# The last tile's second and third column groups stored by one transfer per queue

## The chip, the cores and the metric

The kernel runs on one core of one Trainium2 chip. The metric is the device time of one execution in microseconds (us), as the median of several runs. Beside it stands the span of a profiled execution, from its first to its last instruction; it is about 1.8 us shorter than the time of the same run. The document also uses a third measure, the **tail**: from the end of the last copy out of PSUM to the end of the span, read from the trace.

## The reference

An attention without softmax feeds a gated feed-forward block:

```python
scores = scale * np.matmul(q, k.transpose(0, 1, 3, 2))     # 8 x 12 heads, 448 x 64
attn   = np.maximum(scores, 0.0) ** 2 / S
x      = (attn @ v), heads side by side                     # 3584 x 768
out    = (gelu(x @ w_gate) * (x @ w_val)) @ w_out           # 768 -> 1536 -> 768, float32
```

Only the last step matters here. Its output, 3584 rows of 768 columns, is made in 28 tiles of 128 rows; a tile holds two chunks of 64 rows.

## The kernel before

A planner in the kernel lists operations per engine with their dependencies and emits them in the order of a simulated clock. The part that the change touches makes one column group of one output tile: 48 matmuls into a PSUM bank, a copy to SBUF (`osb`), and the stores. An ordinary tile has two groups of 384 columns; the last tile (`last`) has three, of 384, 192 and 192.

```python
def add_out(at, t, g):
    last = 2 * t + 2 == B * SC
    bounds = (0, OGS, OGS + OGS // 2, 2 * OGS) if last else (0, OGS, 2 * OGS)
    cols = slice(bounds[g], bounds[g + 1])
    ...                                             # matmuls
    def emit_store(j, engine, cols):                # 64 rows of chunk j
        b, c = chunks[j]
        rows = out[b * S:(b + 1) * S, :].rearrange("(p c) d -> c p d", c=SC)
        engine.dma_start(rows[c, :, cols], osb[t][HALF[j], cols])
    ...
    cp = Op("DVE" if last else "ACT", 0.48, emit_copy, [ops[1][-1]], prio=1)
    ...
    if last:
        SP.append(Op("SP", 0.6, lambda: emit_store(0, nc.sync, cols), [cp], prio=-1))
        ACT.append(Op("ACT", 0.1, lambda: emit_store(1, nc.scalar, cols), [cp], prio=-1))
    elif g == NG - 1:
        SP.extend(Op("SP", 0.6, lambda j=j: emit_store(j, nc.sync, slice(0, d_model)), [cp], prio=-1)
                  for j in range(2))
```

So the last tile is stored by six transfers: after each group's copy one from SyncE's queue (SP, chunk 0) and one from ScalarE's queue (ACT, chunk 1), 96, 48 and 48 KB each. An *issue* is what an engine's sequencer, which takes the engine's instructions in order, does to start a transfer; SPq and ACTq in the views below are the sequencers of SyncE and ScalarE. A transfer has *landed* when its semaphore, a counter that the program can wait for, says so.

## Time and profile before

| | before |
|---|---|
| time, median of 3 runs | 429.53 us (429.22 to 430.35) |
| span of the profiled run | 427.8 us |
| TensorE busy | 421.0 us (98%) |
| end of the last matmul / of the last copy | 423.61 / 423.99 us |
| tail (last copy to end of span) | 3.79 us |

The table is read from the bottom. TensorE is busy nearly throughout, so the body is matmul work. The change cannot touch it; it works in the 3.79 us after the last copy, in which the last stores are issued, move their data and land, and the program closes. The prediction shows the lines of this stretch. One more view belongs to them: what SyncE's sequencer waited for from 420 us on (waiter, releaser: us in total, times, longest).

```profile
...
SPq L560 <- DVE osb L555: 2.2, 1, 2.2
SPq L728 <- DMA out_dram<-osb: 1.3, 3, 0.5
SPq L728 <- PEq L728: 0.7, 2, 0.5
```

L728 is the line of the launch; instructions under it are the closing steps that the program adds after the kernel's own. SyncE stands there waiting for landings of `out_dram`, so the landing of the last store and not an engine's work is what the end waits for.

### The profile page before, as it was taken

Reading aid. Unit: us, or ns where it says so; the run is one execution under the profiler, and the core shown is the slowest. Engines: PE = TensorE matmul, PEld = TensorE weight load, DVE = VectorE, ACT = ScalarE, POOL = GpSimd, SP = SyncE. Lnnn points to the kernel's source line nnn. Section 1 sums busy time; section 2 is a strip of 40 time slices with the busy share of each in tenths; the row PEclk is TensorE's granted clock in tenths of the full one; section 3 lists DMA queues with packets and bytes.
Section 4 is the critical chain, followed back from the end, with each engine's and each line's share of the span. In section 5 each row is a group of like instructions: output and inputs, shape, how many; then the busy total and the mean of one; then the engine's idle time right before and its main releaser. Section 6 shows DMA issues by size and latency. Waiting matters only on the chain.

```text
span 427.8 us, 19598 instructions
## 1 busy us (share of the span) xinstructions
PE 421.0 (98%) x9090; PEld 359.3 (84%) x9093; DVE 213.1 (50%) x347; ACT 223.6 (52%) x320; POOL 71.5 (17%) x116
## 2 busy tenths in 40 slices
PE   8999999999999999999999999999999999999996
PEld 3556788789998888889999988979999988977895
DVE  3965766367653665346643566445743555212201
ACT  4946674366655555556465565555546555322220
POOL 7655320012200132012300123011310000000000
PEclk9999999999999999999999999999999999999998
DMA  7999999988964389545975379735984100120034
GB/s 103 190 199 198 201 209 192 139 126 109 121 128 89 47 114 116 118 83 81 133 119 113 48 92 130 149 63 57 137 142 96 38 4 3 48 69 3 2 77 113
DMA packets 75377, 44.91 MB, mean 105 GB/s; under 512 B 36128, under 2 KB 71840, under 8 KB 75296
## 3 DMA queue, kind: packets, MB, share of 16 engines
q0 software_dynamic: 37088, 24.39, 42.1%
q1 hardware_dynamic: 37968, 19.08, 25.9%
q8 instruction: 71, 1.16, 1.2%
q10 hardware_dynamic: 240, 0.20, 0.2%
q14 instruction: 10, 0.08, 0.1%
HBM read 48.76 MB, written 11.01 MB: 140 GB/s over the span
## 4 chain that ended last, share of the span: by engine, by line
PE 96%; DMA 1%; POOL 1%; issue 1%; ACT 0%; DVE 0%; ACTq 0%; POOLq 0%
PE ff L159 86%; PE sp L159 8%; DMA qk<-in_k_dram 1%; PE sp L342 1%; POOL qk L211 1%; PE ff L304 1%; ACT rl L389 0%; PE ff L342 0%; DVE osb L555 0%; POOL ident masks.py:199 0%; POOL ident masks.py:197 0%; ACTq L389 0%; POOLq L717 0%
## 5 line engine op out<-in xcount | busy, mean ns | idle before, releaser
L159 PE MATMUL ff<-xT,wg 64*64 64x448 bf16 x2304 | 217.7, 349 | 0.0
L159 PE MATMUL ff<-xT,wv 64*64 64x448 bf16 x2304 | 216.7, 349 | 0.3 <-issue 0.2
L389 ACT ACTIVATE rl<-sp 128x896 bf16<-128x896 f32 x168 | 152.4, 918 | 94.1 <-PE sp L159 77.2
L159 PE MATMUL ff<-wo,uT 64*64 64x384 bf16 (+1 forms) x2736 | 151.6, 320 | 0.0
L159 PEld LDWEIGHTS <-wv 64*64 64x64 bf16 x2304 | 126.6, 107 | 17.5 <-issue 2.7
L159 PEld LDWEIGHTS <-wg 64*64 64x64 bf16 x2304 | 126.5, 107 | 16.6 <-issue 0.6
L395 DVE TENSOR_TENSOR attnT<-rl 128x896 bf16<-128x896 bf16 x168 | 103.8, 622 | 69.3 <-ACT rl L389 68.2
L159 PEld LDWEIGHTS <-uT 64*64 64x64 bf16 x2736 | 126.8, 107 | 5.1 <-issue 0.3
L159 PE MATMUL sp<-qkT 64*64 64x448 bf16 (+1 forms) x768 | 108.3, 328 | 0.5 <-ACT rl L389 0.4
L503 DVE TENSOR_TENSOR uT<-gel,ff 128x448 bf16<-128x448 bf16 x96 | 59.5, 620 | 79.3 <-PE ff L159 68.8
L159 PE MATMUL ff<-attnT,v 64*64 64x448 bf16 (+1 forms) x768 | 86.0, 326 | 0.1
L498 ACT ACTIVATE gel<-ff 128x448 bf16<-128x448 f32 x96 | 52.1, 543 | 55.2 <-PE ff L159 54.7
L159 PEld LDWEIGHTS <-qkT 64*64 64x64 bf16 x768 | 44.2, 106 | 9.6 <-issue 4.2
L159 PEld LDWEIGHTS <-v 64*64 64x64 bf16 x768 | 46.5, 107 | 5.3 <-issue 1.3
L555 ACT COPY osb<-ff 128x384 f32<-128x384 f32 x54 | 25.7, 476 | 46.6 <-PE ff L159 44.0
L448 DVE TENSOR_SCALAR xT<-ff 128x448 bf16<-128x448 f32 x48 | 29.9, 623 | 31.8 <-PE ff L159 31.7
L211 POOL DMA_DIRECT2D qk<-in_q_dram x25 | 15.5, 622 | 129.3 <-DVE uT L503 121.7
L224 POOL DMA_DIRECT2D v<-in_v_dram x44 | 27.3, 627 | 41.5 <-DVE uT L503 32.0
L211 POOL DMA_DIRECT2D qk<-in_k_dram x25 | 15.4, 615 | 64.0 <-DVE uT L503 55.7
L258 DVE COPY qkr<-qk 128x1792 bf16<-128x1792 bf16 x18 | 19.3, 1077 | 0.0
L555 DVE COPY osb<-ff 128x192 f32<-128x192 f32 (+1 forms) x3 | 1.2, 420 | 18.3 <-PE ff L159 18.3
L342 PEld LDWEIGHTS <-qk 128*64 128x64 bf16 x168 | 5.2, 110 | 3.8 <-issue 3.5
(23 smaller groups left out, 43.9 us busy)
## 6 DMA issues: line engine op xcount, KB each, us to landing
out_dram<-osb SPq DMA_DIRECT2D x54, 192.0 KB, 2.8
v<-in_v_dram POOLq DMA_DIRECT2D x42, 128.0 KB, 4.4
qk<-in_q_dram POOLq DMA_DIRECT2D x23, 224.0 KB, 4.3
qk<-in_k_dram POOLq DMA_DIRECT2D x23, 224.0 KB, 5.1
wg<-in_moe_w_gate_dram POOLq DMA_DIRECT2D x6, 384.0 KB, 10.5
wv<-in_moe_w_val_dram POOLq DMA_DIRECT2D x6, 384.0 KB, 11.3
wo<-in_moe_w_out_dram POOLq DMA_DIRECT2D x4, 576.0 KB, 15.5
v<-in_v_dram POOLq DMA_DIRECT2D x2, 384.0 KB, 11.2
```

Source lines behind the costliest of these rows:

```text
L159: return nc.tensor.matmul(o, lhsT, rhs, start=start, stop=stop, tile_position=(P * row, P * col))
L211: op = load(4 * (h1 - h0) * S * D, lambda: nc.gpsimd.dma_start(tile_of().rearrange("p (h x) -> p h x", h=H)[:, h0:h1, :], src[b, h0:h1].re ...
L224: return nc.gpsimd.dma_start(v16[b][HALF[i], h0:h1, :, :], v[b, h0:h1].rearrange("h (p c) d -> p h c d", c=SC)[:, :, c0:c0 + VC, :])
L258: nc.vector.tensor_copy(qkr[b][:, m], qk16[b].rearrange("p (h c d) -> p c h d", c=SC, d=D)[:, :, 4 * m:4 * m + 4])
L304: nc.tensor.matmul(t[:, :], warm[:, 0:128], warm[:, :], start=True, stop=True)
L342: nc.tensor.transpose(t[HALF[j], c, :], src[:, 2 * (2 * m + r) + j, c, :], ident[:, :], tile_position=(0, P * j))
L389: nc.scalar.activation(rl[:, :, :], box[0][:, :, 0:S], AF.Relu)
L395: nc.vector.tensor_tensor(a[:, :, :], box[1][:, :, :], box[1][:, :, :], op=ALU.mult)
L448: nc.vector.tensor_scalar_mul(xT[b][:, pr, :], box[0][:, 0:S], scalar1=out_scale)
L498: nc.scalar.activation(gel[b, fc][:, :], box[0][:, 0:S], AF.Gelu)
L503: u_op[b, fc].ins = nc.vector.tensor_tensor(uT[b][:, fc, :], gel.pop((b, fc))[:, :], box[0][:, 0:S], op=ALU.mult).ins
L555: (nc.vector.tensor_copy if last else nc.scalar.copy)(osb[t][:, cols], box[0][:, 0:N])
```

## The change

Intent: with one issue less per queue at the end, the last store should leave earlier. The first group is stored as before; the second is not stored on its own, and its columns go out with the third's.

```diff
-        if last:
-            SP.append(Op("SP", 0.6, lambda: emit_store(0, nc.sync, cols), [cp], prio=-1))
-            ACT.append(Op("ACT", 0.1, lambda: emit_store(1, nc.scalar, cols), [cp], prio=-1))
-        elif g == NG - 1:
+        if last and g != 1:
+
+            part = slice(bounds[g and g - 1], bounds[g + 1])
+            SP.append(Op("SP", 0.6, lambda: emit_store(0, nc.sync, part), [cp], prio=-1))
+            ACT.append(Op("ACT", 0.1, lambda: emit_store(1, nc.scalar, part), [cp], prio=-1))
+        elif g == NG - 1 and not last:
```

## The prediction

> **What bounds the kernel now.** I read the page first, then the chain of waits near the end, the timeline of the last five microseconds cut into short windows, the DMA issues of the same windows, and the trace's records of single DMA packets.
>
> ```profile
> span 427.8 us, 19598 instructions
> PE 421.0 (98%) x9090; PEld 359.3 (84%) x9093; DVE 213.1 (50%) x347; ACT 223.6 (52%) x320; POOL 71.5 (17%) x116
> ```
>
> TensorE is busy for 421.0 of 427.8 us, so the body is bound by it. The change does not touch the body; only what follows the last matmul can move. The chain of waits in the window 423 to 428 us (start, us, what):
>
> ```profile
> 422.99 0.62 PE ff L159 x15
> 423.61 0.02 issue
> 423.63 0.36 DVE osb L555
> ```
>
> The last 15 matmuls end at 423.61, the last PSUM copy (192 columns, third group) ends at 423.99, and the chain view stops there. The span ends at 427.77, 3.78 us later, and all of that is the last stores and the program's closing steps. The timeline of this stretch (start, us, engine) and, below it, the DMA issues:
>
> ```profile
> 422.77 0.56 DVE L555 COPY osb<-ff 128x384 f32<-128x384 f32 x1 [18.27 <-PE ff L159]
> ...
> 423.25 0.35 DVE L555 COPY osb<-ff 128x192 f32<-128x192 f32 x1
> ...
> 423.36 0.47 SPq L560 DMA_DIRECT2D out_dram<-osb  x1
> 423.36 0.56 ACTq L560 DMA_DIRECT2D out_dram<-osb  x1
> ...
> 423.63 0.36 DVE L555 COPY osb<-ff 128x192 f32<-128x192 f32 x1
> ...
> 423.92 0.54 SPq L560 DMA_DIRECT2D out_dram<-osb  x1
> ...
> 424.01 0.73 ACTq L560 DMA_DIRECT2D out_dram<-osb  x1
> ...
> 424.56 0.55 SPq L560 DMA_DIRECT2D out_dram<-osb  x1
> 424.83 0.56 ACTq L560 DMA_DIRECT2D out_dram<-osb  x1
> ```
> ```profile
> out_dram<-osb SPq DMA_DIRECT2D x1, 96.0 KB, 2.1
> out_dram<-osb ACTq DMA_DIRECT2D x1, 96.0 KB, 2.4
> ...
> out_dram<-osb SPq DMA_DIRECT2D x1, 48.0 KB, 1.9
> out_dram<-osb ACTq DMA_DIRECT2D x1, 48.0 KB, 2.0
> ```
> ```profile
> L728 SPq EVENT_SEMAPHORE  x4: 17/22/28, 426.8 to 427.7; - x4
> ```
>
> The thing to see is the gap between the copies and the issues. The three copies end at 423.33, 423.60 and 423.99. The first pair of issues follows its copy by 0.03 us. The second copy, though, has been done since 423.60 while the second issues begin at 423.92 (SP) and 424.01 (ACT), each when its sequencer has finished the one before. The third pair is later still: its copy ended at 423.99, but SP issues at 424.56 (0.57 us late) and ACT at 424.83 (0.84 us late). One issue costs a sequencer 0.47 to 0.73 us plus some 0.1 us before the next, while the last two copies come only 0.28 and 0.39 us after their predecessors. Two queues with three issues each therefore cannot keep up. ACT's third store is last: issued at 424.83, 2.0 us to landing. SyncE's wait for it ends at 426.8, and from there 0.97 us of closing semaphores lead to 427.77.
>
> **What the Trainium skill says.** "DMA: Bandwidth & Descriptors", section "Issuing engines are not separate DMA queues": transfers begun from several engines run on the same 16 DMA engines and interleave, and a second issuing engine saves only the sequencer's time to issue. This is the quantity at stake here, and 0.47 to 0.73 us an issue is not small beside a 48 KB transfer. The same page, "Queues, rings and completion order": SP and ACT own one row of rings each, and an engine takes the descriptors of a ring in order. The packet records agree: ACT's second transfer sends its first packet at 425.416, just after its first transfer's last has ended at 425.402; SP's does so at 425.230 after 425.151. The same page, "Anatomy of one DMA", gives about 2.0 us fixed plus bytes over 436 GB/s, most of the fixed part being the receipt of the write; it is written for the other issue path. Here 48 KB takes 1.9 to 2.0 us, which fits the sum, but not its split: the third stores wait 1.22 us (SP) and 1.23 us (ACT) from issue to first packet, and ACT's landing is seen 0.37 us after its last packet ended at 426.437. "Perfetto Trace Analysis", "DMA Instruction — HWDGE": an issue's profiled span runs from satisfied semaphores to the free sequencer, and the movement of data comes outside it. The trace agrees: ACT's third issue ends at 425.39, its packets start at 426.06.
>
> **The change part by part.** Removed: the second group's two issues, one on SP and one on ACT. A comparison of the built instruction streams shows one issue less on each, and no other instruction moved or changed. Copies, matmuls and the first group's stores stay. The last issue now moves 384 columns (96 KB) instead of 192 (48 KB).
>
> 1. *Earlier issue.* SP is free at 423.83 and ACT at 423.92, both before the last copy ends at 423.99. With the 0.03 us seen between the first copy and its issue, both begin at about 424.03 (up to 424.06). For ACT that is 424.83 - 424.03 = 0.80 us earlier, for SP 0.53 us. The second group's data leaves some 0.1 us later than before on SP, and this does not matter.
>
> 2. *Later start of data within the transfer.* From 424.03, 1.23 us to the first packet gives 425.26. On SP its first transfer's packets end at 425.15, so SP starts at about 425.26. On ACT the first transfer's packets occupy the ring to 425.40, so ACT starts at about 425.42, not 425.26. Before, the first packet of ACT's last store was at 426.06; the gain at this point has shrunk from 0.80 to 0.64 us.
>
> 3. *Twice the data at the end.* Two 96 KB transfers now run beside each other. The first group's pair is the same case already measured: first packet 424.483, last end 425.402, so 0.92 us for both, the second having joined 0.45 us late. Its 128 data packets have median lengths of 0.111 (SP) and 0.065 us (ACT), so 64 x 0.111 + 64 x 0.065 = 11.3 us of engine time, or 0.70 us over 16 engines if none idles. My estimate for the new pair is therefore 0.70 to 0.92 us after 425.26, an end of the last packet between 425.96 and 426.18, against 426.44 before. Of the 0.64 us, 0.26 to 0.48 us remain.
>
> 4. *Landing and close.* Plus 0.37 us to the seen landing: 426.33 to 426.55 in place of 426.80. Check by the other route: ACT's 96 KB store of the first group took 2.4 us from issue to landing, and 424.03 + 2.4 = 426.43. The 0.97 us of closing semaphores remain. Two landings less to wait for saves nothing, because those waits were passed earlier.
>
> Sum: -0.80 (issue) + 0.16 (ring still in use) + about 0.27 (more data) = -0.37 us. The span becomes 427.4, and the time 429.53 - 0.37 = 429.16, which I round to 429.15: a gain of 0.09%.
>
> **The rivals.** *The larger transfer gives all of it back.* If two 96 KB transfers together took as long as a full 192 KB store (median 2.8 us to landing in the page's DMA list), landing would be at 424.03 + 2.8 = 426.83, and the time would stay at 429.5. For it: the packets of the first pair were longer than those of 48 KB (0.111 and 0.065 against 0.036 to 0.053 us). Against it: the full stores come two behind each other on one queue, 384 KB in all; here the pair is 192 KB and half of it on each queue. I give this 15%.
>
> *The whole issue gain stays.* If the data were hidden and landing took 2.0 us as for 48 KB, landing would be at 426.03 and the time at 428.76. For it: SP's 96 KB store took only 2.1 us, and the DMA engines were only half busy from 425.5 on. Against it: ACT's took 2.4 us, and the kernel ends with the later of the two. I give 15%.
>
> *Something else sets the end.* The preceding tile's second store on SP, 192 KB, keeps sending single packets until 424.39 in this trace, 0.09 us before SP's next data starts. A later straggler would delay SP's last store through its ring in either kernel; this widens the range but leans to neither side. TensorE cannot become a different bound, as its stream is unchanged.
>
> **Range and chances.** The mechanism allows a gain of 0 to 0.8 us. The three runs of before lie between 429.22 and 430.35, so the scatter of a median of a few runs is as large as the effect. I take 428.65 to 429.75 to hold 8 in 10. 2% would be 8.6 us, more than twice the 3.78 us between the last copy and the end, so faster by 2% cannot come from this change, and nothing in it could cost 8 us. Chances: 0.005 faster, 0.99 same, 0.005 slower.
>
> **What would show it.** In the changed profile: two issues per queue, the second at 424.0 to 424.1 us on both, if the last copy ends again at 423.99 (step 1); first packets of ACT's last store close behind its first store's end (step 2); 96 KB last issues of 2.1 to 2.5 us to landing (step 3); the landing wait ending 0.3 to 0.5 us earlier relative to the last copy, with 0.97 us after it (step 4). The prediction is wrong if the distance from the last copy to the end stays 3.78 us or falls below 3.1 us, or if a last issue takes over 0.8 us because it handles more bytes.

## The result, and the profile after

| | before | after |
|---|---|---|
| time, median of 6 runs each | 429.44 us (428.44 to 430.35) | 429.0 us (428.47 to 429.34) |
| span of the profiled run | 427.77 us | 427.40 us |
| end of the last copy | 423.99 us | 423.76 us |
| tail | 3.79 us | 3.65 us |

The ratio of the times is 0.9988, with a 95% interval of 0.9972 to 1.0003: the same, by any useful standard. A ratio here is the mean time of one kernel's fast runs over that of the other's of the same rounds (in a round the kernels are run in turn), so it is not quite the ratio of the medians in the table. All runs of both kernels were fast, that is, none was an execution at a lower clock.

The median fell by 0.44 us and the profiled span by 0.37, which is just what was predicted. The next two rows show that this agreement is not to be trusted: the last copy itself ended 0.23 us earlier, in a part of the program in which no instruction was changed. Only 0.14 us of the 0.37 lie in the tail.

Where do the other 0.23 us come from? Eleven traces hold the same 9090 matmul records. I took from each the start of the 2727th (30% of them) and of the last. The 2727th starts anywhere from 138.00 to 139.98 us, in kernels that are alike up to there; from it to the last matmul it is 283.98 us in all eleven. So the program's first 140 us scatter by 2 us from run to run, and from there it repeats to 0.01 us. (The other three traces hold three records more, so that the 2727th is another matmul; they are left out.) The tail does so nearly as well. The first copy of the last tile starts 1.21 us before the end of the last copy in every trace, and the two traces of the changed kernel have tails of 3.65 and 3.62 us. Tails of the same kernel differ by up to 0.07 us (see the last experiment), so an effect of 0.14 us is read better from the tails of single traces than from the times of many runs; the kernel before has one trace only.

The timeline of the changed kernel's last microseconds (start, us, engine), the lines that answer to those in the prediction:

```profile
422.54 0.56 DVE L555 COPY osb<-ff 128x384 f32<-128x384 f32 x1 [18.28 <-PE ff L159]
...
423.13 0.47 SPq L560 DMA_DIRECT2D out_dram<-osb  x1
...
423.13 0.56 ACTq L560 DMA_DIRECT2D out_dram<-osb  x1
...
423.40 0.36 DVE L555 COPY osb<-ff 128x192 f32<-128x192 f32 x1
423.78 0.47 SPq L560 DMA_DIRECT2D out_dram<-osb  x1
423.79 0.72 ACTq L560 DMA_DIRECT2D out_dram<-osb  x1
```

Both last issues now start 0.03 us after the last copy (423.40 + 0.36). The queues have stopped being late; the intent of the change is met in full. The DMA issues of the window after the copy (queue, count, KB, us from issue to landing), then what SyncE waited for from 422 us on, then SyncE's closing semaphore instructions from the last landing on:

```profile
out_dram<-osb SPq DMA_DIRECT2D x1, 96.0 KB, 2.3
out_dram<-osb ACTq DMA_DIRECT2D x1, 96.0 KB, 2.5
```
```profile
SPq L560 <- DVE osb L555: 2.2, 1, 2.2
SPq L730 <- DMA out_dram<-osb: 1.8, 3, 0.9
SPq L730 <- PEq L730: 0.7, 2, 0.5
```
```profile
L730 SPq EVENT_SEMAPHORE  x6: 17/28/28, 426.3 to 427.3; - x6
```

(L730 is the same line of the launch, two lines lower.) Two things differ from what was expected. ACT's last store takes 2.5 us and not 2.4. And after the last landing, at 426.3, SyncE still has six semaphore instructions to do, where the kernel before had four after 426.8.

ACT's last store, the last to land in both, in numbers from the two traces; times are us after the end of the last copy. Those of packets, here and below, are from the traces' records of single DMA packets, which no view prints:

| | before | after | moved by |
|---|---|---|---|
| issue starts | 0.85 | 0.03 | -0.82 |
| first data packet | 2.08 | 1.63 | -0.44 |
| last data packet ends | 2.45 | 2.19 | -0.25 |
| SyncE's wait for it ends | 2.82 | 2.56 | -0.26 |
| end of span | 3.79 | 3.65 | -0.14 |

The 0.82 us that the issue won shrink at each row: 0.37 us are lost between issue and first packet, 0.19 in the longer movement of data, and 0.12 after the landing.

### The profile page after: what moved, and what is told of

It reads as the page before. It is cut to its first block, busy times and chain, and to the rows that moved or that the text cites. A ratio compares the mean times of both kernels' runs of the same rounds, so it can differ in the third digit from the quotient of the medians.

```text
span 427.4 us, 19594 instructions
## 1 busy us (share of the span) xinstructions
PE 421.1 (99%) x9090; PEld 359.7 (84%) x9093; DVE 213.1 (50%) x347; ACT 223.5 (52%) x320; POOL 71.5 (17%) x116
## 4 chain that ended last, share of the span: by engine, by line
PE 98%; ACT 0%; issue 0%; DVE 0%; ACTq 0%
PE ff L159 86%; PE sp L159 8%; PE ff L304 1%; PE ff L699 1%; PE sp L342 1%; PE ff L342 1%; ACT rl L389 0%; DVE osb L555 0%; DVE warm L145 0%; DVE table L148 0%; ACTq L389 0%
## 5 line engine op out<-in xcount | busy, mean ns | idle before, releaser
L159 PEld LDWEIGHTS <-uT 64*64 64x64 bf16 x2736 | 128.7, 107 | 3.9
```

Of the source, the lines that this page charges most:

```text
L159: return nc.tensor.matmul(o, lhsT, rhs, start=start, stop=stop, tile_position=(P * row, P * col))
```

## The experiments

The main theory, the prediction's: the sequencers' issues set the end, and a merged store wins their time back less what a larger transfer costs. Its rivals: the number of transfers or of bytes decides, whichever queue they are on. From the result came two further questions: what holds ACT's first packet back, and why the closing takes 0.12 us longer. All times below are tails unless another thing is named. The runs that were made for their trace alone have one time each, between 427.9 and 429.7 us, which within the scatter of the program's start says nothing.

### Twice the issues: quarters

The base is the kernel before; the second and third groups are each stored in two halves, five issues per queue.

```diff
-            SP.append(... emit_store(0, nc.sync, cols) ...)
-            ACT.append(... emit_store(1, nc.scalar, cols) ...)
+            mid = (bounds[g] + bounds[g + 1]) // 2
+            for c in ((cols,) if g == 0 else (slice(bounds[g], mid), slice(mid, bounds[g + 1]))):
+                SP.append(... emit_store(0, nc.sync, c) ...)
+                ACT.append(... emit_store(1, nc.scalar, c) ...)
```

> Measure: the tail, from the end of the last PSUM copy to the end of the span (3.79 us in the kernel before, 3.65 in the changed one). Here the issues after the first group are doubled: 5 per queue, each 96 columns (24 KB). Theory (sequencer time per issue sets when the last store leaves): ACT's issues followed each other by 0.65 and 0.82 us in the kernel before, so its fifth begins about 2.2 to 2.4 us after the last copy in place of 0.85, lands about 2.0 us later, and the tail is about 5.2 to 5.4 us. Rival (the movement of bytes and the landing set the end, issues are hidden): the bytes are the same, the tail stays within 0.1 of 3.8 us.

Measured: tail 5.22 us, 1.44 us over the kernel before, with the same bytes. The timeline from 424.7 us on (the last copy ended at 422.62):

```profile
424.43 0.59 SPq L560 DMA_DIRECT2D out_dram<-osb  x1
424.71 0.61 ACTq L560 DMA_DIRECT2D out_dram<-osb  x1
```

ACT's fifth issue begins 2.09 us after the copy, in place of 0.85 for its third. The theory holds and the rival falls: issues on a queue are in line, each at 0.6 to 0.8 us, and they set the end once there are too many. The expected 2.2 to 2.4 us for the issue was a little too much. That the tail still fell in the expected 5.2 to 5.4 us has some luck in it: SyncE's wait for the last landing ends 1.20 us later than before, and the other 0.24 us of the 1.44 come after it, where the close takes 1.21 us in place of 0.97. The closing list, below, explains this.

### One queue alone: act_merged, sp_merged

The base is the kernel before; one of the two appends is left as it was, and the other is made for groups 0 and 2 only, as in the change.

```diff
 # act_merged
             SP.append(... emit_store(0, nc.sync, cols) ...)
-            ACT.append(... emit_store(1, nc.scalar, cols) ...)
+            if g != 1:
+                part = slice(bounds[g and g - 1], bounds[g + 1])
+                ACT.append(... emit_store(1, nc.scalar, part) ...)
 # sp_merged: the same with the two queues exchanged
```

> Only ACT's second and third store are merged; SP keeps three. Theory of the issue queue: ACT's third issue was the last of all (0.85 us after the last copy), so merging it alone gives most of the gain; SP's third issue still comes about 0.57 us after the copy, 48 KB, lands about 1.95 us later, at 2.5 us after the copy (2.82 before, 2.56 in the changed kernel). Tail 3.5 to 3.65 us. Rival (both merges count equally): tail about halfway, 3.7 us.

> Only SP's second and third store are merged; ACT keeps three and its third issue is still the last. Theory of the issue queue: nothing gained, ACT's last issue again about 0.85 us after the copy and the last landing about 2.8 us after it, tail 3.7 to 3.9 us. Rival (fewer transfers in all is what helps, whichever queue): tail about 3.7 us or less, ACT's last landing at 2.7 us or earlier.

Measured: 3.63 us with ACT merged, 3.84 with SP merged. The last issue of each, SP's third with ACT merged (the last copy ended at 424.27) and ACT's third with SP merged (424.08):

```profile
424.84 0.55 SPq L560 DMA_DIRECT2D out_dram<-osb  x1
```
```profile
424.93 0.57 ACTq L560 DMA_DIRECT2D out_dram<-osb  x1
```

The merge on SP alone gives nothing: ACT's third store, issued at 0.85 us as before, is waited for until 2.87 us after the copy (2.82 in the kernel before). The merge on ACT alone moves the end of the last wait to 2.67 us (expected 2.5), where it is that for SP's third store; with both merged it is 2.56. So ACT's merge gives 0.15 of the 0.26 us won at the landing, and SP's gives the other 0.11, but only once ACT's has been made. That the tail with ACT alone merged is as short as with both, 3.63 against 3.62 and 3.65, comes from the stretch after the landing: 0.97 us there, 1.09 with both merged. In sum, fewer transfers do not help unless they are on the queue that is last. The 0.05 us that SP's merge alone seems to cost are no more than tails scatter (up to 0.07 us, as the last experiment shows).

### All bytes at the end: one_pair

The base is the changed kernel; all three groups go out after the last copy, 192 KB per queue.

```diff
-        if last and g != 1:
-            part = slice(bounds[g and g - 1], bounds[g + 1])
+        if last and g == 2:
+            part = slice(0, d_model)
```

> All three groups go out in one pair of 192 KB stores after the last copy. Theory: fewest issues but all bytes at the end. First packets 1.13 (SP) and 1.57 us (ACT) after the issue as in the first pair of both kernels; data of 384 KB takes about 1.4 to 1.6 us against 0.94 for the changed kernel's last pair; last landing about 3.0 us after the copy and tail about 4.1 us. Rival (fewer issues is always better): tail at or below 3.65 us.

Measured: 4.43 us, so fewer issues are not always better. The DMA issues after the last copy:

```profile
out_dram<-osb SPq DMA_DIRECT2D x1, 192.0 KB, 2.7
out_dram<-osb ACTq DMA_DIRECT2D x1, 192.0 KB, 3.2
```

The expected 4.1 us was missed. About 0.1 us of the miss lies after the landing (1.21 us, as in quarters, where the changed kernel has 1.09); the rest, a last wait that ends at 3.22 us and not at 3.0, was the first hint at the loss between issue and first packet. The two issues start 0.004 us apart, yet ACT's first packet comes 2.14 us after its issue and not 1.57. SP's comes after 1.12 us, and its data runs until 2.39 us after the copy. ACT's first packet stood behind most of SP's.

### What holds ACT's first packet back: sp_tiny, sp_tiny4, sp_late, ring_free

These four give a wrong result: part of the output is left unwritten, so that bytes can be taken away while the issues stay. The base is the changed kernel, in which ACT's first packet comes 1.60 us after its issue.

```diff
 # sp_tiny: SP's last store is the first 8 columns of its 384
+            few = part if g == 0 else slice(part.start, part.start + 8)
-            SP.append(... emit_store(0, nc.sync, part) ...)
+            SP.append(... emit_store(0, nc.sync, few) ...)
 # sp_tiny4, in emit_store: SP's last store is 4 pieces of 8 columns a row
+            if last and g and j == 0:
+                dst = dst.rearrange("p (n x) -> p n x", n=4)[:, :, 0:8]   # and src alike
 # sp_late: as sp_tiny, but the last 8 columns
+            few = part if g == 0 else slice(part.stop - 8, part.stop)
 # ring_free: as sp_late, and ACT's first store is 8 columns too
+            ACT.append(... emit_store(1, nc.scalar, few if g == 0 else part) ...)
```

> Wrong result on purpose: SP's last store moves 8 of its 384 columns (2 KB in all, still 64 pieces), ACT's is whole. Question: in the changed kernel the two last issues begin at the same moment, but ACT's first packet comes 1.60 us after its issue and SP's 1.23 us. Theory (bytes: ACT's packets stand behind SP's on the same 16 DMA engines): without SP's bytes ACT's first packet comes 1.2 to 1.35 us after its issue, its last ends about 1.8 us after the copy in place of 2.19, and the tail is 3.2 to 3.35 us in place of 3.65. Rival (the two issues share one descriptor path, which takes about 0.4 us for 64 pieces whatever their size): ACT's first packet still comes 1.55 to 1.65 us after its issue, and the tail is 3.5 us or more.

> Wrong result on purpose: SP's last store moves 4 x 8 columns a row, 256 pieces of 32 bytes (8 KB in all) in place of 64 pieces of 1536 bytes. Theory (bytes): ACT's first packet within 0.2 us of that in the run with 64 tiny pieces. Rival (shared descriptor path, cost by pieces): it moves later by about 3 x 0.4 = 1.2 us. If both hold, it lies between: the bytes explain the run with 64 pieces, the pieces the difference of the two.

> Wrong result on purpose. The run with SP's tiny last store left a confusion: its 8 columns belonged to the second group, so SP issued 0.09 us before ACT and not beside it. Here SP's last store is the last 8 columns (64 pieces, 2 KB), so both issues begin at the same moment again. If SP's bytes hold ACT's packets back: ACT's first packet 1.39 to 1.45 us after its issue (its own ring is busy until then). If two issues at the same moment share a path at a fixed cost, whatever their bytes: 1.55 to 1.65 us after, as in the changed kernel and in the run with 256 tiny pieces.

> Wrong result on purpose. As the run before it, and ACT's first store too moves only 8 columns, so ACT's ring is free long before its last store. If the ring was the floor of 1.39 to 1.41 us: ACT's first packet now 1.22 to 1.3 us after its issue. If a fixed cost of two issues at once is the floor: 1.55 to 1.65 us in this run and in the one before it. If neither: as in the run before it, 1.39 to 1.45 us.

| | SP's last store | ACT's issue to its first packet | tail |
|---|---|---|---|
| changed kernel, two traces | 64 pieces, 96 KB | 1.60 and 1.56 us | 3.65 and 3.62 us |
| sp_tiny | 64 pieces, 2 KB, issued 0.09 us before ACT | 1.41 us | 3.42 us |
| sp_tiny4 | 256 pieces, 8 KB | 1.58 us | 3.67 us |
| sp_late | 64 pieces, 2 KB | 1.40 us | 3.49 us |
| ring_free | 64 pieces, 2 KB; ACT's ring free | 1.40 us | 3.49 us |

The first run of the four was muddled: its 8 columns were of the second group, so SP no longer issued at the same moment. Its tail of 3.42 us lay between what the two theories asked for, and 0.06 us of it were won after the landing (1.03 us in place of 1.09). sp_late mends this. With both issues again at once and only SP's bytes gone, the delay falls from 1.56 or 1.60 to 1.40 us; so a fixed price of two issues at once is not the cause of this part, and 0.16 to 0.20 us of the delay are SP's data on the shared DMA engines. (Three more traces below, of sems2 and sems3, have the same two stores and delays of 1.55 to 1.61 us.) With half of SP's data, 48 KB, issued 0.09 us before ACT, nothing is added: the delay is 1.39 us in act_merged, and 1.40 us for ACT's second store in the kernel before. sp_tiny4 adds that many small pieces hold ACT back as well as few large ones: 256 pieces of 32 bytes give 1.58 us, though they are a twelfth of the bytes. So it is not the bytes alone; the 0.31 us in which those pieces run on the engines would explain it, but no run separates this further. It also shows that pieces do not cost 0.4 us per 64, as the rival had it: the delay would have grown by over a microsecond.

The remaining 1.40 us were expected to be ACT's own ring (its queue's line of pieces on the DMA engines, taken in order as the prediction has it), which is busy with its first store until about 1.42 us after the copy. ring_free refutes this. There the ring is empty from 1.15 us on, and the delay is 1.40 us all the same. The timeline of sp_late after its last copy (423.29) suggests where to look. ACT's second issue lasts 0.72 us,

```profile
423.32 0.47 SPq L560 DMA_DIRECT2D out_dram<-osb  x1
423.33 0.72 ACTq L560 DMA_DIRECT2D out_dram<-osb  x1
```

as ACT's second issue does in all 13 traces that have one (0.72 to 0.73 us, each with an issue of SP's less than 0.1 us from it), while ACT's third issue in the kernel before lasts 0.56 us and has its first packet after 1.23 us. 0.72 - 0.56 = 0.16 us, and 1.40 - 1.23 = 0.17 us. Counted from the end of the issue, the first packet comes 0.67 to 0.68 us later in both, and 0.66 to 0.67 us later for ACT's four issues after the first in quarters. So the floor goes with the longer issue. Why ACT's second issue is longer, when its first, equally beside one of SP's, is 0.56 us, no run here tells; a price of two issues at once is not excluded for these 0.16 us.

### The closing list: sems2, sems3

In the traces SyncE's closing instructions check semaphores in a fixed order, and the eight that the stores use in turn are checked from the first to the last, one every 0.06 us if nothing is to be waited for. In the kernel before, ACT's last store has the seventh. With two transfers fewer it has the fifth, and two more checks come behind it: 2 x 0.062 = 0.124 us, the amount lost. To test this, the stores of an early tile (20) are cut in pieces, so that the turn stands two or three further at the end.

```diff
-            SP.extend(Op("SP", 0.6, lambda j=j: emit_store(j, nc.sync, slice(0, d_model)), [cp], prio=-1)
-                      for j in range(2))
+            for j in range(2):
+                n = 2 if t == 20 else 1          # sems3: n = 2 + j if t == 20 else 1
+                SP.extend(Op("SP", 0.6, lambda j=j, i=i, n=n: emit_store(
+                    j, nc.sync, slice(i * d_model // n, (i + 1) * d_model // n)), [cp], prio=-1)
+                          for i in range(n))
```

> The changed kernel with the stores of an early tile (number 20) cut into two column halves each, two transfers more, so that the round of eight semaphores stands two further at the end. Theory (closing list): the last landing, ACT's, is checked as the 7th of the list's eight store semaphores in place of the 5th; from the wait that ends last to the end of the span 0.97 us as in the kernel before, in place of 1.09; tail 3.52 us. Rival (the closing stretch differs for another cause, such as two transfers fewer): it stays 1.09 us and the tail 3.65 us.

> The changed kernel with three transfers more at tile 20, so that ACT's last store has the last semaphore of the closing list and SP's the first. Theory: from the wait that ends last to the end 0.91 us, tail 3.46 us, so 0.19 us below the changed kernel and 0.33 below the one before; in the time of the runs about 0.9992 of the kernel before, not clear of the scatter. Rival: tail 3.65 us as in the changed kernel.

Measured: 3.53 us for sems2, with 0.97 us from the last landing to the end: the lost 0.12 us are back. SyncE's semaphore instructions from the last landing on are four again:

```profile
L733 SPq EVENT_SEMAPHORE  x4: 17/22/28, 425.2 to 426.1; - x4
```

sems3 missed: 3.66 us in place of 3.46. ACT's last store has the last semaphore there, as wanted, but SP's has the first, and it lands late too, 2.32 us after the copy. All seven other checks then stand behind it:

```profile
L733 SPq EVENT_SEMAPHORE  x10: 17/28/28, 426.9 to 428.2; - x10
```

The last check is made at 2.75 us, though ACT's data had ended at 2.21. The rule of the list is thus wider than I had it: each landing costs its own time plus one check for every semaphore behind it, and the largest of these sums ends the list. The other traces fit it: from the wait for the last landing to the end of the span it is 1.21 us where that store has the third semaphore (quarters, one_pair), 1.09 with the fifth (1.06 in the changed kernel's second trace), 1.03 with the sixth (sp_tiny) and 0.97 with the seventh, 0.06 us a place. sems3 was also timed in five rounds: 429.81 us median (6 runs), ratio 1.0005, interval 0.9983 to 1.0027.

### The times again: after_again, sems2_timed

> The changed kernel again, for the repeat of its tail and for its time in five rounds. Theory: tail 3.65 us within 0.02 as in its first trace, so 0.14 us below the kernel before; the end of the last copy scatters by several tenths of a microsecond from run to run, so the ratio is 0.999 to 1.000 with an interval that holds 0.9997 (0.14 of 429.4 us). Rival (the 0.37 us of the two profiled spans belong to the change): tail about 3.4 us, or an interval wholly below 0.9996.

> The kernel with the two extra transfers at tile 20 again, for its time. Tail 3.53 us within 0.02, as in its first trace (changed kernel 3.62 to 3.65, kernel before 3.79). 0.26 us of 429.3 is 0.0006, below what five rounds resolve (the start-up of the program scatters by about 2 us in the traces so far): ratio 0.998 to 1.0015, interval holding 1. If it were a real gain of over 0.5 us elsewhere, the interval would lie below 0.999.

The changed kernel in five rounds: 428.98 us (6 runs, 428.09 to 430.33) against 429.16 us for the kernel before (11 runs, 428.46 to 431.29), ratio 0.9989, interval 0.9966 to 1.0011; tail 3.62 us, just outside the promised 0.02. The interval holds both 0.9997, which the tail implies, and the 0.9991 of the prediction. The times do not decide between them.

sems2 in five rounds: 428.57 us (427.48 to 429.78) against 429.47 us (11 runs, 428.02 to 430.98), ratio 0.998, interval 0.9954 to 1.0005; tail 3.46 us. This tail is 0.07 us shorter than in its first trace, since ACT's data ended that much earlier; such is the scatter of a tail. It is the shortest of all kernels with a right result, 0.25 to 0.32 us below the kernel before. The median difference of 0.9 us is not shown to be real: the interval holds 1, and the tail accounts for a third of it.

## Why the prediction was right, and where it was not

The time of 429.0 us lies in the range, next to the predicted 429.15, and the class "same" is right. The frame that led there also holds: only the 3.78 us after the last copy could move, and so 2% was out of reach. But the central figure, a gain of 0.37 us, was met by chance. The tail shows 0.14 us (0.16 in the second trace); the rest of the span's 0.37 us came from the scatter of the program's start.

**Step 1 was right.** Both last issues start 0.03 us after the copy; ACT's was won 0.82 us, predicted 0.80. The runs with twice the issues and with one queue merged show that this is the mechanism, and that ACT's queue comes first: its merge gives 0.15 us of the landing alone, SP's nothing without it and 0.11 us with it. (The second copy ends 0.27 us after the first, not 0.28 as the prediction has it; nothing hangs on it.)

**Step 2 named the wrong cause, and its amount was too small.** It let ACT's first packet wait for ACT's own ring until 1.39 us after the issue. It came after 1.60 us. With the ring free the delay is 1.40 us all the same, so the ring was not the floor. The trace of the kernel before had this delay already, 1.40 us for ACT's second store; since its packets began just as those of the first store had ended, the prediction read it as the ring's order. And a further 0.16 to 0.20 us are SP's data, which the step did not count at all. What had to be kept was a gain of 0.64 us at this point; 0.44 remained.

**Step 3 had the mechanism, and its estimate was slightly low.** The two stores took 0.94 us from SP's first packet to ACT's last, and the estimate was 0.70 to 0.92. Part of what step 2 missed was hidden in this span, since it had been measured on the first pair, where ACT's packets stand behind SP's too. That is why the landing, at 2.56 us after the copy, is at the late end of the predicted 2.35 to 2.57 and not beyond it: 0.26 us were won, where the sum had counted on 0.37 and the prediction's signs on 0.3 to 0.5.

**Step 4 failed.** It held the close at 0.97 us and said that two landings less to wait for saves nothing. It is 1.09 us (1.06 in the second trace): fewer transfers moved the last store to an earlier place in the closing list, and the checks behind it cost 0.12 us. sems2 shows this by giving them back.

Of the rivals, "the larger transfer gives all of it back" did not come true: it put the landing 2.84 us after the copy, and it came at 2.56. But more was given back than the sum had: 0.56 of the 0.82 us up to the landing, and 0.12 in the close, which no rival had. "The whole issue gain stays" was refuted by the same landing. A late straggler on SP's ring was not tried: the preceding tile's last packet ended 0.40 to 0.43 us after the last copy wherever the traces let it be told apart, and SP's first data packet came at 0.50 to 0.51 us in every kernel that stores the first group early.

## What to carry to other kernels

At the end of a program count the issues per queue against the distance of the copies that release them: an issue of 0.5 to 0.7 us on the queue that is last is on the path, and one on the other queue costs nothing until that queue becomes the last. Merging stores trades these issues for bytes that move after the last copy, so most of the gain can go again, and fewer transfers may shift which semaphore the closing waits check last. Where a program's start scatters by more than the effect, compare a stretch of the trace that begins after the scatter, and distrust a total that agrees with the prediction.

## What the Trainium skill lacked or had wrong

- "DMA: Bandwidth & Descriptors", section "Specifications", gives about 0.6 us to the first byte for transfers issued from SP or ACT. From the start of the issue it was 1.13 to 1.31 us on SP and 1.23 to 1.60 us on ACT, for the last tile's stores in the kernel before and the changed one; counted from the end of the issue it was 0.66 to 0.77 us on SP, and 0.67 to 0.68 us on ACT for the second and third store of the kernel before (0.88 to 1.02 us for the ACT stores issued together with 96 KB of SP's). The page does not say from where it counts.
- The same page, section "Issuing engines are not separate DMA queues", calls the sequencer's time to issue usually small relative to the DMA itself. Here an issue took 0.47 to 0.73 us, while the last 48 KB stores took 1.95 us from issue to landing, 0.37 us of it for their packets; doubling the issues with the bytes kept put off the last landing by 1.20 us. It has no figure for how long the second of two stores issued together waits for the first: 0.16 to 0.20 us with 96 KB before it, and a first packet 2.14 us after the issue with 192 KB.
- No page has the order of the closing checks: one semaphore each 0.06 us in a fixed list, which made the close 0.97 to 1.34 us (the latter in sems3, 3.66 - 2.32) according to the place of the landing that held it up.
